# A fused attention and expert kernel: first batch in a new order, fourth batch later, a fourth buffer of scaled q, a third early unit of x sums

## The chip, the cores and the metric

One core of one Trainium2 chip. Times are device microseconds (us) of a whole execution. A ratio is the mean time of one kernel's fast runs over that of the other's fast runs of the same rounds, with a 95% interval, so it is not quite the ratio of the medians that are quoted. Times in a profile count from the start of its span, which is about 1.7 us shorter than the execution's time.

## The reference, cut to what matters

```python
# q, k, v: (8 batches, 8 heads, 576 positions, 64)
q_p = concat(relu(q) * cos, relu(q) * sin)        # the "scaled q", k_p likewise
kv  = einsum('bhsf,bhsd->bhfd', k_p, v);  z = k_p.sum(axis=2)
num = einsum('bhsf,bhfd->bhsd', q_p, kv)
den = einsum('bhsf,bhf->bhs', q_p, z)[..., None] + 1e-6
x   = (num / den) as (4608, 512)
P   = exp(x @ w_gate), 8 Sinkhorn rounds
out = sum over 8 experts e of P[:, e] * (relu(x @ w1[e]) @ w2[e])   # w1 512x1024, w2 1024x512
```

## The kernel before

TensorE works through expert 0 in blocks j = 0 to 8, each of 16 slots (8 of the first layer, 8 of the second, about 19 us). In the slots of block j the attention of batch b = j + 1 is finished and that of batch j + 2 prepared. After block 6 the buffers of the attention are freed, and experts 1 to 7 follow in a form with fewer products that works on sums of parts of x ("x sums", in units of 2 x 384 tokens). A helper `at(block, slot, fn, ...)` puts a piece of work into a slot. On TensorE, VectorE (DVE) and ScalarE (ACT) the order is the written one.

The denominators need scaled q with its features on the partitions. From batch 2 on that is done by DMA transposes issued by SyncE (SP), one for each pair of heads (hk = 0 to 3), 288 KB each. Loads of q, k and v are issued by GpSimd (POOL), six of 288 KB for a batch.

```python
kp_pool = p1.enter_context(tc.tile_pool(name="kp_pool", bufs=4))
qp_pool = p1.enter_context(tc.tile_pool(name="qp_pool", bufs=3))     # scaled q
rb_pool = p1.enter_context(tc.tile_pool(name="rb_pool", bufs=4))     # spread reciprocals
# ... cut ...
def load(b, half, names="qkv", held_back=False):
    for name in names:
        # ... cut: i = nc.gpsimd.dma_start(...)
        if held_back:
            after(ve.last, i)        # not before the DVE operation written last
        landing[name, b, half] = i

def prep_q(b, hk):
    q16 = loaded.pop(("q", b, hk))
    # ... cut: relu on DVE
    q_p = qp_pool.tile([P, C, 2, D], F16, name="q_p")
    ve.tensor_tensor(out=q_p[:], in0=..., in1=cs, op=ALU.mult)
    if by_dma:                       # b >= 2
        turned = nc.sync.dma_start(out=qTs[b, hk], in_=q_p[:]..., transpose=True)
        if b == 3 and hk == 0:
            after(landing["v", b, 1], turned)
# ... cut ...
for slot, fn, hk in (...) if j == 1 else (
    (4, prep_q, 0), (5, prep_k, 0), (5, prep_q, 1), (6, prep_k, 1),
    (8, prep_q, 2), (8, prep_k, 2), (10, prep_q, 3), (10, prep_k, 3),
    (11, prep_kv, 0), (14, prep_kv, 1),
) if j == 2 else (...):
    at(j, slot, fn, b + 1, hk)
if j == 1:
    for name in "qkv":
        for half in range(2):
            at(j, 12, load, b + 2, half, name, True)
elif j and b + 2 < B:
    for half in range(2):
        at(j, 11 + half, load, b + 2, half, "qkv", True)

def x_sums_early(n):                 # in block 6, saved to DRAM, read back later
    pool, name = ((kp_pool, "k_p"), (qp_pool, "q_p"))[n]
    # ... cut: four DVE operations, three saves
for n in range(2):
    at(B - 2, (2, 5)[n], x_sums_early, n)
```

## Time and profile before

| | before |
|---|---|
| median of 3 runs | 975.6 us (975.55 to 975.99) |
| span of the profiled run, mean clock | 972.1 us, 0.999 |
| TensorE busy | 959.4 us, 99% |
| DVE, ACT busy | 83%, 58% |

TensorE is the bound, and with 1% of idle time a change can win little. The prediction below shows the lines for the bound. Columns: start, length, engine, line, operation, output<-input, in brackets the idle time before and what ended it.

```profile
82.01 0.76 DVE L109 TENSOR_TENSOR q_p<-q_ld,acc_hi 128x1152 f16<-128x1152 f16 x1 [1.23 <-DMA q_pT<-q_p]
...
83.35 0.45 DVE L109 COPY acc_lo<-v_ld 128x576 f16<-128x576 f16 x1
...
84.10 0.72 POOL L233 DMA_DIRECT2D q_ld<-in_q_dram  x1 [13.47 <-DVE acc_lo L109]
```

DVE makes the fourth scaled q of batch 4 only when the first transpose has freed a buffer (82.01), then a copy of v (83.35), and that copy is what the loads of batch 5 are tied to (84.10). At 84.10 the fourth transpose had been issued for 1.3 us. With three buffers the fourth product cannot be made before the first transpose has landed, and the loads of batch 5 come behind that product: so the order of DVE, and the buffer it waits for, keep these loads behind the fourth transpose.

### The profile page before, as it was taken

The numbers are of one execution on the slowest core, as the hardware profiler recorded it, in microseconds if no ns is written. First come the engines' busy times: TensorE is split into PE (matmuls) and PEld (weight loads), VectorE is DVE, ScalarE is ACT, GpSimd is POOL, SyncE is SP. The second block draws the span as 40 slices with busy tenths as digits, with TensorE's granted clock in tenths as the row PEclk, the third lists the DMA queues.
The fourth block names the chain that finished last, engine by engine and source line by source line (L and its number), as shares of the span: only waits on it lengthen the run. The fifth ranks groups of instructions, "written<-read, shape, count | busy, mean of one in ns | idle before, by whom it ended". The sixth has DMA issues, their size and how long they took to land.

```text
span 972.1 us, 20258 instructions
## 1 busy us (share of the span) xinstructions
PE 959.4 (99%) x7855; PEld 674.6 (69%) x7855; DVE 807.4 (83%) x1831; ACT 565.0 (58%) x1264; POOL 60.7 (6%) x82
## 2 busy tenths in 40 slices
PE   9999999999999999999999999999999999999997
PEld 6545555567777777777777777777777777777775
DVE  7767776789898887987888987987888987987887
ACT  5767665577776555555555555555555555555551
POOL 6231210010000000000000000000000000000001
PEclk9999999999999999999999999999999999999999
DMA  9999988231004301332004301322004401115435
GB/s 162 188 154 173 156 137 184 44 69 50 26 26 93 69 25 50 68 62 57 25 26 93 69 25 51 68 54 65 26 25 86 75 25 42 33 28 124 123 90 127
DMA packets 81200, 74.72 MB, mean 77 GB/s; under 512 B 33360, under 2 KB 73040, under 8 KB 81104
## 3 DMA queue, kind: packets, MB, share of 16 engines
q0 software_dynamic: 27232, 30.94, 20.4%
q1 hardware_dynamic: 53632, 42.24, 17.8%
q8 instruction: 61, 1.00, 0.4%
q14 instruction: 35, 0.29, 0.1%
q10 hardware_dynamic: 240, 0.26, 0.1%
HBM read 84.30 MB, written 12.98 MB: 100 GB/s over the span
## 4 chain that ended last, share of the span: by engine, by line
PE 91%; DMA 4%; issue 2%; DVE 1%; POOL 1%; ACT 0%; POOLq 0%; DVEq 0%; SPq 0%; ACTq 0%
PE rows_ps L109 34%; PE h_ps L109 28%; PE p_ps L109 11%; PE copied_ps L109 11%; PE y_ps L109 4%; PE small_ps L109 3%; DMA k_ld<-in_k_dram 1%; DMA w1e<-in_moe_w_dram 1%; DMA w2e<-in_moe_w_dram 1%; DVE acc_hi L975 0%; POOL q_ld L233 0%; POOL hs_last L990 0%; DMA out_dram<-acc_lo 0%; DVE H L905 0%; DVE S L203 0%
## 5 line engine op out<-in xcount | busy, mean ns | idle before, releaser
L975 DVE SCALAR_TENSOR_TENSOR acc_lo<-rows_ps,P_tok,acc_lo 128x512 f32<-128x512 f32 (+1 forms) x322 | 203.8, 642 | 74.9 <-PE rows_ps L109 74.8
L109 PEld LDWEIGHTS <-H 128*128 128x128 f16 x2080 | 203.1, 98 | 82.3 <-issue 1.4
L911 ACT CAST u<-h_ps 128x384 f16<-128x384 f32 x288 | 137.5, 478 | 129.7 <-PE h_ps L109 129.7
L109 PEld LDWEIGHTS <-w1e 128*128 128x128 f16 x1632 | 157.7, 98 | 67.2 <-issue 5.3
L905 DVE CUSTOM_DVE_ANT_0 H<-p_ps,u 128x384 f16<-128x384 f32 x329 | 181.7, 552 | 7.2 <-PE p_ps L109 7.1
L109 PEld LDWEIGHTS <-hs 128*128 128x128 f16 x1500 | 146.6, 98 | 56.2
L109 PE MATMUL p_ps<-xT,T 128*128 128x384 f16 x672 | 164.2, 326 | 1.0 <-DVE H L905 0.9
L109 PE MATMUL h_ps<-S,w1e 128*128 128x384 f16 x672 | 164.2, 326 | 0.8 <-ACT u L911 0.6
L109 PE MATMUL rows_ps<-V,H 128*128 128x256 f16 x1000 | 150.0, 273 | 0.7 <-DVE acc_hi L975 0.7
L109 PE MATMUL rows_ps<-w2e,hs 128*128 128x256 f16 x1000 | 150.0, 273 | 0.0
L109 PE MATMUL h_ps<-xT,w1e 128*128 128x384 f16 (+1 forms) x616 | 148.8, 351 | 0.1
L943 ACT ACTIVATE H<-h_ps 128x384 f16<-128x384 f32 x144 | 70.6, 490 | 94.5 <-PE h_ps L109 94.5
L109 PEld LDWEIGHTS <-T 128*128 128x128 f16 x1008 | 98.4, 98 | 31.9 <-issue 4.9
L109 PE MATMUL rows_ps<-w2e,H 128*128 128x256 f16 (+1 forms) x568 | 94.4, 285 | 0.0
L924 ACT COPY copied_ps<-h_ps 128x384 f32<-128x384 f32 x144 | 67.5, 469 | 36.0 <-PE h_ps L109 35.2
L934 ACT ACTIVATE H<-copied_ps 128x384 f16<-128x384 f32 x144 | 70.8, 492 | 20.4 <-PE copied_ps L109 20.4
L109 PE MATMUL h_ps<-S,T 128*128 128x384 f16 x336 | 81.8, 325 | 0.6 <-ACT copied_ps L109 0.5
L109 PE MATMUL copied_ps<-xT,w1e 128*128 128x384 f16 x336 | 82.1, 326 | 0.0
L109 PE MATMUL copied_ps<-w2e,H 128*128 128x256 f16 x504 | 75.6, 273 | 0.0
L109 PE MATMUL rows_ps<-V,hs 128*128 128x256 f16 x500 | 75.0, 273 | 0.0
L975 DVE SCALAR_TENSOR_TENSOR acc_lo<-copied_ps,P_tok,acc_lo 128x256 f32<-128x256 f32 x126 | 60.3, 479 | 0.4
L975 DVE SCALAR_TENSOR_TENSOR acc_hi<-rows_ps,P_tok,acc_hi 128x512 f32<-128x512 f32 (+1 forms) x56 | 41.4, 739 | 20.6 <-PE rows_ps L109 19.7
(146 smaller groups left out, 947.7 us busy)
## 6 DMA issues: line engine op xcount, KB each, us to landing
S<-x_saved SPq DMA_DIRECT2D x114, 192.0 KB, 2.4
out_dram<-acc_lo SPq DMA_DIRECT2D x62, 128.0 KB, 2.4
w1e<-in_moe_w_dram POOLq DMA_DIRECT2D x7, 1024.0 KB, 8.8
w2e<-in_moe_w_dram POOLq DMA_DIRECT2D x7, 1024.0 KB, 9.6
q_ld<-in_q_dram POOLq DMA_DIRECT2D x16, 288.0 KB, 6.5
k_ld<-in_k_dram POOLq DMA_DIRECT2D x16, 288.0 KB, 7.8
v_ld<-in_v_dram POOLq DMA_DIRECT2D x16, 288.0 KB, 9.6
x_saved<-S SPq DMA_DIRECT2D x12, 192.0 KB, 1.8
```

What stands on the lines that cost most here:

```text
L109: i = getattr(self.engine, name)(*args, **kwargs)
L905: latest = ve._custom_dve(TENSOR_ADD_SAT, out=out, in0=ps[:, 0:TU], in1=t[:], s0=FP32_MAX, s1=0.0)
L911: se.copy(out=t[:], in_=ps[:, 0:TU])
L924: se.copy(out=Y[:, 0:TU], in_=X[:, 0:TU])
L934: se.activation(out=h11, in_=Y[:, 0:TU], func=AF.Relu)
L943: se.activation(out=h12, in_=X[:, 0:TU], func=AF.Relu)
L975: ve.scalar_tensor_tensor(out=a, in0=rows, scalar=P_tok[:, g, self.e : self.e + 1], in1=a, op0=ALU.mult, op1=ALU.add,)
```

## The change

Its intent: (A) bring the first batch to the matmuls earlier; (B) move the preparation of batch 3, the "fourth batch", later, because ACT stood at its k near 58 us, and let the loads of batch 4 follow its transposes; (C) a fourth buffer of scaled q, paid for with one of rb; (D) make the x sums of a third unit in block 6. Under (B) the preparation of batch 4 in block 2 moves to later slots too.

```diff
 C
-        qp_pool = ... bufs=3          rb_pool = ... bufs=4
+        qp_pool = ... bufs=4          rb_pool = ... bufs=3
 B
+        turnings = {}
-        def load(b, half, names="qkv", held_back=False):
+        def load(b, half, names="qkv", held_back=False, behind=None):
-                if held_back:
+                if behind is not None:
+                    after(turnings[behind], i)
+                elif held_back:
-                if b == 3 and hk == 0:
+                if b == 3:
                     after(landing["v", b, 1], turned)
+                turnings[b, hk] = turned
@@ preparation of batch 3 in block 1: k at slots 9, 10, 12, 13 (were 8, 9, 10, 12); kv of hk 0 and 1 at 13, 14 (were 10, 12)
@@ j == 2: kv of hk 2 and 3 at slots 0 and 1 (were in block 1)
@@ sums of batch 3 both at block 2, slot 2 (were block 1, slot 15 and block 2, slot 0)
@@ denominators of batch 3 at slot 4 (was 3)
@@ preparation of batch 4 in block 2
-                    (4, prep_q, 0), (5, prep_k, 0), (5, prep_q, 1), (6, prep_k, 1),
-                    (8, prep_q, 2), (8, prep_k, 2), (10, prep_q, 3), (10, prep_k, 3),
+                    (5, prep_q, 0), (6, prep_q, 1), (8, prep_k, 0), (8, prep_q, 2),
+                    (9, prep_k, 1), (10, prep_q, 3), (10, prep_k, 2), (11, prep_k, 3),
-                        at(j, 12, load, b + 2, half, name, True)
+                        at(j, 12, load, b + 2, half, name, True, (b + 1, HK - 1))
 D
-        for n in range(2):
-            at(B - 2, (2, 5)[n], x_sums_early, n)
+        for n in range(3):
+            at(B - 2, (2, 5, 9)[n], x_sums_early, n)
@@ in expert 1 the third unit is read back instead of made in place
 A (cut: some 120 lines)
+        load(0, 1, "q")               # ahead of the iota
@@ filler of the start: 110 x 64 columns instead of 74 x 128
@@ denominators ahead of the last k product, numerators interleaved with the first layer
```

More of the change, by code (lines that the diff above doesn't have):

```diff
@@ L214 @@
         kp_pool = p1.enter_context(tc.tile_pool(name="kp_pool", bufs=4))
-        qp_pool = p1.enter_context(tc.tile_pool(name="qp_pool", bufs=3))
+        qp_pool = p1.enter_context(tc.tile_pool(name="qp_pool", bufs=4))
         qT_pool = p1.enter_context(tc.tile_pool(name="qT_pool", bufs=1))
         kv_pool = p1.enter_context(tc.tile_pool(name="kv_pool", bufs=2))
-        rb_pool = p1.enter_context(tc.tile_pool(name="rb_pool", bufs=4))
+        rb_pool = p1.enter_context(tc.tile_pool(name="rb_pool", bufs=3))
         cs_pool = p1.enter_context(tc.tile_pool(name="cs_pool", bufs=1))
@@ L253 @@
         )
+        load(0, 0, "k")
         ones_sq = cs_pool.tile([P, P], F16, name="ones_sq")
@@ L261 @@
         )
-        load(0, 1, "q")
-        for name in "kv":
-            load(0, 0, name)
-            load(0, 1, name)
+        load(0, 1, "k")
+        for half in range(2):
+            load(0, half, "v")
         w0 = new_weights(wA)
@@ L287 @@
         idle_ps = ps_y.tile([P, Dm], FP32, name="y_ps")
-        for _ in range(74):
-            keep_busy(1)
+        for _ in range(110):
+            te.matmul(
+                out=idle_ps[:, 0:HP], lhsT=ones_sq[:],
+                rhs=ones_sq[:, 0:1].to_broadcast([P, HP]), start=True, stop=True,
+            )
         wrap = cs_pool.tile([P, C], FP32, name="wrap")
@@ L306, with halve @@
         ve.memset(cs_half[:], 0.0)
-        for hh in range(2):
-            ve.tensor_copy(
-                out=cs_half[hh * HP : (hh + 1) * HP, :, :, hh],
-                in_=cs[hh * HP : (hh + 1) * HP, :, :, 0],
-            )
+        def halve():
+            for hh in range(2):
+                ve.tensor_copy(
+                    out=cs_half[hh * HP : (hh + 1) * HP, :, :, hh],
+                    in_=cs[hh * HP : (hh + 1) * HP, :, :, 0],
+                )
         early = cs_pool.tile([P, 1], FP32, name="early")
@@ L320 @@
         C3 = C // 3
+        ones_col = const.tile([P, 1], FP32, name="ones_col")
+        ve.memset(ones_col[:], 1.0)
+        ones_all = const.tile([P, P], FP32, name="ones_all")
+        ve.memset(ones_all[:], 1.0)
+        eps_row = cs_pool.tile([1, 32], FP32, name="eps_row")
+        ve.memset(eps_row[:], 1e-6 / XS)
+        lent = acc_lo[:, G_LO - 4 : G_LO, :].rearrange("p g d -> p (g d)").bitcast(F16)
+        VA = C * (D + 2)
+        v_augs = [
+            lent[:, i * VA : (i + 1) * VA].rearrange("p (c d) -> p c d", d=D + 2)
+            for i in range(4)
+        ]
+        for t in v_augs:
+            ve.memset(t[:, :, D : D + 1], 1.0 / XS)
         lo = cs_pool.tile([P, 1], FP32, name="lo")
@@ L339 @@
         )
-        ones_col = const.tile([P, 1], FP32, name="ones_col")
-        ve.memset(ones_col[:], 1.0)
-        ones_all = const.tile([P, P], FP32, name="ones_all")
-        ve.memset(ones_all[:], 1.0)
-        eps_row = cs_pool.tile([1, 32], FP32, name="eps_row")
-        ve.memset(eps_row[:], 1e-6 / XS)
         wg_ld = cs_pool.tile([P, KT, E], FP32, name="wg_ld")
@@ L352 @@
         kps, qps, qTs, kvs, hls = {}, {}, {}, {}, {}
-        lent = acc_lo[:, G_LO - 4 : G_LO, :].rearrange("p g d -> p (g d)").bitcast(F16)
-        VA = C * (D + 2)
-        v_augs = [
-            lent[:, i * VA : (i + 1) * VA].rearrange("p (c d) -> p c d", d=D + 2)
-            for i in range(4)
-        ]
         q_pTs = [qT_pool.tile([P, C, P], F16, name=f"q_pT{i}")[:] for i in range(6)] + [
@@ L366 @@
         ]
-        for t in v_augs:
-            ve.memset(t[:, :, D : D + 1], 1.0 / XS)
         def prep_k(b, hk, by_scalar=True):
@@ L475, in sums, with sums_begun @@
             sums_made(b, half, sums_begun(b, half))
-        def sums_begun(b, half):
+        def sums_begun(b, half, banks=(ps_s, "small_ps")):
             W_ = D + 1 if b else D
@@ L484, in sums_begun @@
                 )
-            kv_ps = [ps_s.tile([P, 512], FP32, name="small_ps") for hh in range(2)]
+            kv_ps = [banks[0].tile([P, 512], FP32, name=banks[1]) for hh in range(2)]
             for i in range(2):
@@ L643 @@
         for hk in range(HK):
+            prep_q(0, hk)
+            if hk == 1:
+                halve()
             if hk == 3:
@@ L647 @@
                 z_ps = key_sums(0)
-                prep_q(0, hk)
-                key_sums_made(0, z_ps)
-            else:
-                prep_q(0, hk)
             for i in range(3):
                 turn(0, hk, i, True)
-                keep_busy(3)
+                keep_busy(3 * (hk < 3))
         prep_kp(0, 0)
+        key_sums_made(0, z_ps)
+        for hk in (2, 3):
+            prep_k(0, hk)
         prep_kp(0, 1)
         denominators(0, range(0, 4))
-        keep_busy(8)
-        for hk in (2, 3):
-            prep_k(0, hk)
         z_ps = key_sums(1)
+        keep_busy(4)
+        key_sums_made(1, z_ps)
         prep_kp(0, 2)
-        key_sums_made(1, z_ps)
+        denominators(0, range(4, 8))
         prep_kp(0, 3)
-        keep_busy(5)
-        denominators(0, range(4, 8))
-        for half in range(2):
-            sums_made(0, half, sums_begun(0, half))
-            keep_busy((0, 18)[half])
+        sums_made(0, 0, sums_begun(0, 0))
+        keep_busy(20)
+        spread_out(0, 0)
+        numerators(0, 0)
+        keep_busy(4)
+        spread_out(0, 1)
+        sums_made(0, 1, sums_begun(0, 1, (ps_h[0], "h_ps")))
         hT = hA.tile([P, FT, TCH], F16, name="hT")
@@ L676, with first_l1 @@
         ]
-        for hk in range(HK):
-            attend(0, hk)
-            for kt in ((), (0,), (1,), (2, 3))[hk]:
-                for ft, h_ps in enumerate(first_ps):
-                    te.matmul(
-                        out=h_ps[:],
-                        lhsT=w0[0][:, kt, ft * P : (ft + 1) * P],
-                        rhs=xT[:, kt, 0:TCH],
-                        start=(kt == 0),
-                        stop=(kt == KT - 1),
-                    )
-                    if kt == KT - 1:
-                        se.activation(out=hT[:, ft, 0:TCH], in_=h_ps[:], func=AF.Relu)
-            for i in ((), (0,), (1, 2), ())[hk]:
-                prep_k(1, i, i < 2)
-            for i in ((), (0,), (1,), (2, 3))[hk]:
-                if i == 3:
-                    prep_k(1, i, False)
-                prep_kp(1, i)
+        def first_l1(kt, fts):
+            for ft in fts:
+                te.matmul(
+                    out=first_ps[ft][:],
+                    lhsT=w0[0][:, kt, ft * P : (ft + 1) * P],
+                    rhs=xT[:, kt, 0:TCH],
+                    start=(kt == 0),
+                    stop=(kt == KT - 1),
+                )
+                if kt == KT - 1:
+                    se.activation(out=hT[:, ft, 0:TCH], in_=first_ps[ft][:], func=AF.Relu)
+        numerators(0, 1)
+        spread_out(0, 2)
+        first_l1(0, (2, 3, 0, 1))
+        numerators(0, 2)
+        spread_out(0, 3)
+        first_l1(1, range(4))
+        numerators(0, 3)
+        prep_k(1, 0)
+        prep_k(1, 1)
+        first_l1(2, range(4))
+        first_l1(3, range(4))
+        for hk in range(HK):
+            if hk >= 2:
+                prep_k(1, hk, False)
+            prep_kp(1, hk)
         for hk in range(3):
@@ L707 @@
                     for i in range(3):
-                        at(0, (5, 6, 6, 7)[hk], turn, 1, hk, i, i != 1)
+                        at(0, (6, 6, 7, 7)[hk], turn, 1, hk, i, i != 1)
                     if hk == 0:
-                        at(0, 5, prep_q, 1, 3)
-                    if hk == 2:
-                        at(0, 6, prep_v, 1, 0, se.copy)
-                        at(0, 6, prep_v, 1, 2, ve.tensor_copy)
-                    if hk == 3:
-                        at(0, 7, prep_v, 1, 1, se.copy)
-                        at(0, 7, prep_v, 1, 3, ve.tensor_copy)
+                        at(0, 6, prep_q, 1, 3)
+                    if hk in (1, 3):
+                        for i in (hk - 1, hk):
+                            at(0, (6, 7)[hk // 2], prep_v, 1, i, ve.tensor_copy)
                 for half in range(2):
@@ L737 @@
                     at(j, 5, sums, b, 1)
-                elif j == 2:
-                    at(j, 0, sums, b, 1)
                 else:
@@ L744 @@
                     at(j, 2, sums, b, 1)
-                at(j, 6 if j == 1 else 3 if j == 2 else 4, denominators, b)
+                at(j, 6 if j == 1 else 4, denominators, b)
                 for hk in range(HK):
@@ L765 @@
                 for slot, fn, hk in (
-                    (4, prep_q, 0), (5, prep_q, 1), (8, prep_k, 0), (8, prep_q, 2),
-                    (9, prep_k, 1), (10, prep_kv, 0), (10, prep_k, 2), (12, prep_q, 3),
-                    (12, prep_kv, 1), (12, prep_k, 3), (13, prep_kv, 2), (14, prep_kp, 3),
-                    (14, prep_v, 3),
+                    (4, prep_q, 0), (5, prep_q, 1), (9, prep_k, 0), (8, prep_q, 2),
+                    (10, prep_k, 1), (12, prep_q, 3), (12, prep_k, 2), (13, prep_k, 3),
+                    (13, prep_kv, 0), (14, prep_kv, 1),
                 ) if j == 1 else (
-                    (4, prep_q, 0), (5, prep_k, 0), (5, prep_q, 1), (6, prep_k, 1),
-                    (8, prep_q, 2), (8, prep_k, 2), (10, prep_q, 3), (10, prep_k, 3),
+                    (5, prep_q, 0), (6, prep_q, 1), (8, prep_k, 0), (8, prep_q, 2),
+                    (9, prep_k, 1), (10, prep_q, 3), (10, prep_k, 2), (11, prep_k, 3),
                     (11, prep_kv, 0), (14, prep_kv, 1),
@@ L779 @@
                     at(j, slot, fn, b + 1, hk, *((se.copy,) if fn is prep_v else ()))
-                if j == 1:
-                    at(j, 15, sums, b + 1, 0)
             if j == 1:
@@ L789, in x_sums_early @@
         def x_sums_early(n):
-            pool, name = ((kp_pool, "k_p"), (qp_pool, "q_p"))[n]
+            pool, name = ((kp_pool, "k_p"), (qp_pool, "q_p"))[n % 2]
             ts = [pool.tile([P, C, 2, D], F16, name=name) for _ in range(3)]
@@ L1219 @@
                 m = (n + 1) % NU
-                if e == 1 and m:
-                    if n == 0:
-                        xs_next = xs_first[1]
-                        continue
+                if e == 1 and n == 0:
+                    xs_next = xs_first[1]
+                    continue
+                if e == 1 and m > 2:
                     if i == 0:
@@ L1233 @@
                     if not (e == E - 1 and m == 0):
-                        x_again(m, xs_next)
+                        x_again(m, xs_next, saved[-1] if e == 1 and m == 2 else None)
                 if e > 1 and n == 0 and i == 0:
```

## The prediction

> **What bounds the kernel now.** I read the page first (busy times, slices), then the table of stages, then the waits of TensorE, and then the order of time around each wait.
>
> ```profile
> PE 959.4 (99%) x7855; PEld 674.6 (69%) x7855; DVE 807.4 (83%) x1831; ACT 565.0 (58%) x1264; POOL 60.7 (6%) x82
> ```
>
> ```profile
> 24.00:36.00 12.00, 10.48 (x159) 6.40 (x159) 8.10 (x18) 9.28 (x22) 4.50 (x7) 1.00 1.22 206
> 36.00:56.00 20.00, 20.00 (x225) 10.30 (x224) 17.74 (x38) 12.96 (x30) 4.30 (x6) 1.00 1.06 157
> 56.00:60.00 4.00, 2.83 (x18) 1.15 (x17) 2.04 (x6) 2.11 (x5) 0.00 (x0) 1.00 1.21 167
> 60.00:161.50 101.50, 101.43 (x1066) 52.18 (x1066) 74.59 (x169) 65.88 (x153) 18.89 (x26) 1.00 0.97 161
> 161.50:183.60 22.10, 22.10 (x128) 11.11 (x127) 16.64 (x47) 11.98 (x21) 0.00 (x0) 1.00 0.29 74
> 183.60:198.00 14.40, 13.92 (x80) 7.76 (x79) 10.70 (x25) 9.27 (x20) 0.76 (x1) 1.00 0.43 75
> 198.00:208.00 10.00, 9.01 (x58) 5.41 (x56) 9.44 (x19) 6.20 (x14) 4.03 (x3) 1.00 0.61 116
> 208.00:951.00 743.00, 742.02 (x5661) 553.08 (x5660) 637.02 (x1430) 430.57 (x964) 8.18 (x10) 1.00 0.24 56
> ```
>
> In the stage rows the columns are stretch, length, busy time of PE, weight loads, DVE, ACT, POOL, clock, DMA share, GB/s. From 60 to 161.5 us and from 208 to 951 us the matmul queue is full. The change leaves the matmuls that compute as they are (the build has the same shapes in another order; only filler differs), so it can win only where TensorE is idle or does filler: the start, 24 to 36 (1.52 us idle), 56 to 60 (1.17), 198 to 208 (0.99). A bound from spacing the matmuls at columns / 2.4 per ns says the real losses there are a little larger than the idle time: about 2.8, 1.6 and 1.5 us. Filler of the start is 18,048 columns, 7.5 us, but it fills waits and does not set them.
>
> The wait at 56 to 60:
>
> ```profile
> 57.89 0.68 ACT L109 ACTIVATE k_ld<-k_ld 128x576 f16<-128x576 f16 x1 [2.25 <-DMA k_ld<-in_k_dram]
> ...
> 58.95 0.70 ACT L109 COPY rb<-small_ps 128x384 f32<-128x384 f32 x2
> ...
> 59.48 0.46 PE L109 MATMUL small_ps<-hl,acc_hi 96*128 96x192 f16 x3 [1.11 <-ACT rb L109]
> ```
>
> ACT stands at the relu of the fourth batch's k until the load lands (57.87), with the copies that free the PSUM banks behind it.
>
> **What the Trainium skill says.** "Trainium Kernel Development and Optimization", Key Constraints: DMAs of all issuing queues run on the same 16 engines and interleave; "DMA: Bandwidth & Descriptors", Queues, rings and completion order: an engine round-robins between its queues by packet. The trace agrees: from 156 to 161 us the weights' queue and the save queue alternate, one packet of each per 0.15 us an engine, so the saves move about 150 KB/us, and the weights 115 instead of the 205 that they get alone. "TensorE: Matmul & The Clock Gate", Part 1: after an idle window of about 3.4 us the array falls to half clock, and a busy window brings it back. In this trace the clock records say full speed from 3.95 us to 969.92, 1.85 us after the last matmul ended, so a window that is partly busy can also fall; no wait inside the kernel is long enough to show it.
>
> **The change part by part.**
>
> *Start.* The second half of q is issued before the iota, the spread of cosines to halves is put behind two q products (2 copies, 0.50 us), and the denominators come before the last k product. Before: first q product 6.83, reciprocal 15.50, hl done 17.6. With the durations of before: q product 0.71 each back to back, first at about 6.0 (q landed at 5.95); k relu at about 10.2 (its load landed at 10.47; DMA is saturated, landings come every 1.4 us); 0.55 + 0.70 + 0.29 + 0.55 + 0.70 + 0.29 + 0.70 on DVE and reciprocal at about 14.2; hl done 16.2. Gain 1.4. Then four times copy of rb (0.70 on ACT) and product (0.82 on DVE), with one kv copy (0.5) between, and both engines handing PSUM banks over: last xT about 22.6, before 23.87. After it DVE has four k products, two relus, four q products, four evacuations and four v copies (two of them from ACT), in steps of 0.70, 0.27, 0.70, 0.47, 0.37: 9.5 us, to 32.1; before, the same place waited for ACT's v copy, 32.76. With 36 matmuls of sums (0.6) the first w2 matmul comes at about 32.8, before 33.78. The second w2 piece landed at 31.81, so weights allow it. **Gain 1.0 us** (0.3 to 1.8).
>
> *Fourth batch later.* Its relu of k moves from slot 8 to 9, behind the rb copies, its transposes wait for v, which frees the DMA engines for the loads (one transpose took from 53.64 to 63.81 in that crowd), and the sums of one half move to the next block. I expect the wait at 58 to go: **1.4 us**. The transposes then end about 68, and the denominators want them at about 69.5: no new wait, with 1 us to spare. The fourth scaled-q buffer takes away a DVE wait of 1.23 us at 82.01 that nothing on TensorE waited for: 0.
>
> *Third unit of x sums.* Four DVE operations of 0.55 us leave 198 to 204 and one more copy goes with the others. At 204.3 TensorE waited 0.85 us for an add on DVE, and DVE was busy for 9.44 of 10 us. In the new order another w2 difference (0.68) comes ahead of that add, so of 1.5 us of losses I count **0.8 us**.
> In block 6 the four operations fall in DVE's idle 3.12 us ahead of 159.64: no cost there. But they are saved to DRAM, three saves of 192 KB, and this is where I see the price:
>
> ```profile
> 147.86 1.79 SPq L207 DMA_DIRECT2D x_saved<-k_p  x3
> 152.37 1.51 SPq L207 DMA_DIRECT2D x_saved<-q_p  x3
> 162.62 2.76 SPq L865 DMA_DIRECT2D S<-x_saved  x6
> ...
> 162.67 0.60 ACT L109 ACTIVATE H<-h_ps 128x512 f16<-128x512 f32 x1 [0.35 <-PE h_ps L109]
> ```
>
> The H buffer of the next stage lies where the k and q products lay: in the built program ACT's first write of H waits for every save from them, in both kernels. Before, the sixth landed at 162.49, and H started at 162.67, just as the matmuls had h ready. The new saves are issued at about 157 to 158.5 behind three that end at 162.2; 24 packets an engine at 0.15 us are 3.6 us, so the last lands at about 166.1 on the old clock. TensorE has two h banks: it fills both by 163.75 and stands until the first is read at 166.9. **Loss 3.1 us.** If this wait drops the clock (more likely than not by the 1.85 us above), matmuls of a window of 3.4 us run at half speed: 1 to 1.7 us more, in expectation 0.8.
>
> Sum: 975.6 - 1.0 - 1.4 - 0.8 + 3.1 + 0.8 = 976.3. The order of the fillers looks tuned on the chip, which speaks for more gain at the start than I can trace; I take 1.3 off: **975.0 us**.
>
> **The rivals.** (a) The saves land in time, for instance because they queue more evenly over the engines: then the gains stand alone, 975.6 - 3.2 = 972.4, with a start gain of 2 us 971. For it: the last packets of the saves come from one late engine (most end at 160.9, the last starts at 162.19); against: 3.6 us of packets even on the others end past 164. (b) ACT's wait for k only moves: if the loads of the fourth batch are not faster, ACT stands one slot later; banks are then free for two slots, so at most 0.5 us. (c) The start is bound by loads, not by order: they land every 1.4 us from 5.95 to 43.1 without a break. Then the start gives 0 to 0.3, and with the wait for saves and the clock the time is 977 to 978.5. For it: DMA share 1.2 in this stretch; against: no DVE or TensorE wait after 12 us names a load.
>
> **Range and chances.** Gains 2 to 5 us, losses 0 to 5: 970.8 to 978.6 holds it eight times in ten. Two per cent is 19.5 us, far beyond both.
>
> **What would show it.** Right: ACT's first write of H near 163 to 164 waiting for a save, a TensorE idle of about 3 us after eight matmuls of stage 7, the eight or so 512-column matmuls after it at twice their 0.21 us spacing if the clock fell; the wait of 1.1 us near 57 gone; no wait for DVE near 202. Wrong: the first w2 matmul later than 33.8 or earlier than 31.8, saves that land before h is ready, or a new wait in block 2 for the fourth batch's transposes. The prediction as a whole fails if a wait that I did not find costs more than 5 us, or if the start gains more than 3.

## The result, and the profile after

The kernel after took 989.19 us (990.41, 990.68, 987.25, 987.98), against 975.63 us before in the same rounds: ratio 1.0137, interval 1.0115 to 1.0159. That is within 2%, but 13.6 us slower and far outside the predicted range. Its profiled run took 990.41 us, span 988.7, mean clock 0.992.

The table of stages, columns as in the prediction, first of the kernel before:

```profile
84.00:106.00 22.00, 22.00 (x223) 11.23 (x222) 17.25 (x40) 13.36 (x31) 8.32 (x12) 1.00 1.02 163
...
161.00:183.00 22.00, 22.00 (x128) 11.01 (x126) 16.27 (x47) 11.75 (x21) 0.00 (x0) 1.00 0.32 79
```

and of the kernel after:

```profile
56.00:60.00 4.00, 4.00 (x27) 1.82 (x28) 2.43 (x6) 3.35 (x8) 0.00 (x0) 1.00 1.11 182
...
84.00:106.00 22.00, 12.20 (x148) 5.82 (x147) 9.18 (x22) 6.83 (x15) 3.68 (x6) 0.77 0.87 128
...
161.00:183.00 22.00, 18.40 (x130) 8.96 (x127) 11.61 (x27) 9.69 (x22) 0.00 (x0) 0.92 0.94 227
```

The wait at 56 to 60 is gone, as predicted. From 84 to 106 us TensorE is busy for 12.20 of 22 us, at a clock of 0.77; from 161 to 183 it loses another 3.6 us. The first is the surprise. TensorE in order of time in the kernel after:

```profile
89.90 0.51 PE L109 MATMUL small_ps<-q_pT,zsel 128*32 128x192 f16 x12
91.76 0.34 PE L109 MATMUL small_ps<-q_pT,zsel 128*32 128x192 f16 x6 [1.34 <-DMA q_pT<-q_p]
100.33 0.51 PE L109 MATMUL small_ps<-q_pT,zsel 128*32 128x192 f16 x6 [8.23 <-DMA q_pT<-q_p]
100.77 1.89 PE L109 MATMUL h_ps<-xT,w1e 128*128 128x512 f16 x4
```

The denominators of batch 4 wait 1.34 and 8.23 us for the last two transposes of its scaled q. The clock records say half speed from 95.84 to 106.08 us: four matmuls of 512 columns take 1.89 us instead of 1.04. Of those 10.24 us some 4.5 lie in the wait itself, and in the other 5.7 half the work is lost, 2.9 us. The chain that ended last, cut to this stage (start, length, what), tells why:

```profile
71.99 10.62 DMA v_ld<-in_v_dram
...
82.63 0.04 DVE acc_lo L109
...
85.48 14.81 DMA q_pT<-q_p
100.29 0.04 issue
100.33 0.51 PE small_ps L109 x4
```

A load of v issued at 71.99 lands after 10.6 us, and a transpose issued at 85.48 takes 14.81 us. What ran beside it stands in the order of all engines of the kernel after, to be held against the three lines of before:

```profile
77.79 7.59 SPq L403 DMA_TRANSPOSE q_pT<-q_p  x2
...
78.33 0.76 DVE L109 TENSOR_TENSOR q_p<-q_ld,acc_hi 128x1152 f16<-128x1152 f16 x1
...
82.63 0.45 DVE L109 COPY acc_lo<-v_ld 128x576 f16<-128x576 f16 x1 [2.88 <-DMA v_ld<-in_v_dram]
...
83.39 0.72 POOL L234 DMA_DIRECT2D q_ld<-in_q_dram  x1 [9.97 <-DVE acc_lo L109]
```

With four buffers the fourth scaled q is ready at 79.09 and waits for nothing. But the second transpose holds SP for 5.7 us, so the third is issued at 83.62 and the fourth at 85.48. The copy of v is no longer behind a wait for a transpose; it waits only for its own load, and lets the loads of batch 5 out at 83.39, ahead of both. From issue to landing the transposes took, in the window from 70 to 101 us, in the kernel before (two of batch 5 are counted with it; the four of batch 4 alone took 4.2 to 6.0, median 5.5) and then after:

```profile
DMA to landing us min/median/max: 3.3/4.6/6.0
```

```profile
DMA to landing us min/median/max: 8.1/9.8/14.8
```

The second loss is the one that was predicted, at the first write of H in block 7 (PE in the kernel after):

```profile
178.34 4.13 PE L109 MATMUL h_ps<-xT,w1e 128*128 128x512 f16 x12 [3.60 <-ACT H L109]
```

The saves of the third unit were issued from 167.83 on and landed at 174.55, 175.87 and 177.15; ACT wrote H at 177.69, and the clock was at half from 177.76 to 181.17.

### The profile page after: what moved, and what is told of

It reads as the page before. It is cut to its first block, busy times and chain, and to the rows that moved or that the text cites. A ratio compares the mean times of both kernels' runs of the same rounds, so it can differ in the third digit from the quotient of the medians.

```text
span 988.7 us, 20313 instructions
## 1 busy us (share of the span) xinstructions
PE 963.7 (97%) x7886; PEld 675.5 (68%) x7886; DVE 808.9 (82%) x1834; ACT 564.4 (57%) x1261; POOL 60.7 (6%) x82
## 4 chain that ended last, share of the span: by engine, by line
PE 87%; DMA 7%; DVE 2%; issue 2%; POOL 1%; ACT 0%; SPq 0%; POOLq 0%; DVEq 0%; ACTq 0%
PE rows_ps L109 34%; PE h_ps L109 26%; PE p_ps L109 11%; PE copied_ps L109 11%; PE y_ps L109 3%; PE small_ps L109 2%; DMA q_pT<-q_p 1%; DMA w1e<-in_moe_w_dram 1%; DMA w2e<-in_moe_w_dram 1%; DMA v_ld<-in_v_dram 1%; DMA q_ld<-in_q_dram 1%; DMA k_ld<-in_k_dram 1%; DMA S<-x_saved 0%; DMA acc_hi<-q_p 0%; DVE acc_hi L991 0%
## 5 line engine op out<-in xcount | busy, mean ns | idle before, releaser
L109 PE MATMUL h_ps<-xT,w1e 128*128 128x384 f16 (+1 forms) x616 | 152.4, 357 | 3.7 <-ACT H L109 3.6
L109 PE MATMUL copied_ps<-xT,w1e 128*128 128x384 f16 x336 | 82.1, 326 | 0.0
```

What stands on the lines that cost most here:

```text
L109: i = getattr(self.engine, name)(*args, **kwargs)
```

## The experiments

Eighteen kernels, each beside runs of the kernel before (medians 975.2 to 975.7 us). Issue and landing times are those of the transfers in the trace. The expectations give some waits as the time beyond what the columns of the matmuls need, so they differ by a few tenths of a us from the waits of the trace. This table gathers what the trace says of the kernels that matter for block 3; "b4" is batch 4, the waits are TensorE's in blocks 2 and 3, half clock leaves out the first and last microseconds:

| kernel | loads b4: first issue, last landing | transposes b4: first, last landing | loads b5: first issue | waits of TensorE over 1 us | half clock |
|---|---|---|---|---|---|
| before | 66.33, 80.78 | 81.92, 87.00 | 84.10 | none | none |
| after | 69.14, 84.62 | 85.43, 100.29 | 83.39 | 1.34 + 8.23 (transposes b4) | 10.2 + 3.4 us |
| e1 | 62.45, 79.50 | 87.97, 94.64 | 92.71 | 9.21 (transposes b3) | 13.7 + 3.4 |
| e3 | 69.68, 81.76 | 84.32, 88.44 | 86.51 | 2.24 (DVE, block 2) | 3.4 |
| e5 | 70.01, 85.00 | 85.83, 89.13 | 89.69 | 4.01 (ACT for k) | 3.4 + 3.4 |
| e7 | 66.39, 82.58 | 84.33, 97.70 | 80.43 | 6.72 + 1.25 (transposes b4) | 10.2 + 3.4 |
| e11 | 66.34, 79.74 | 83.29, 86.19 | 84.74 | 1.12 (ACT for k) | none |
| e14 | 66.18, 78.97 | 81.54, 84.75 | 83.02 | none | none |

### First call: undo one part at a time

My first theory was that the hold on the loads of batch 4 (`behind`) made them late, so that they starved the transposes. The rivals were the later slots and the fourth q buffer.

**e1_no_hold**

```diff
-  at(j, 12, load, b + 2, half, name, True, (b + 1, HK - 1))
+  at(j, 12, load, b + 2, half, name, True)
```

> The kernel after, but the loads of batch 4 are no longer held behind the last transpose of batch 3; they wait only for the DVE operation before them in program order, as in the kernel before. Theory (the hold makes the loads of batch 4 late, so that they and then the loads of batch 5 starve the transposes of batch 4, for which the denominators of batch 4 wait 9.6 us in block 3): the loads are issued near 63 us instead of 69.1, all six have landed by about 77, the four transposes of batch 4 land before 88, the wait of 1.34 + 8.23 us and the 10.2 us of half clock after it are gone; a new wait of up to 3 us can come near 70, where the transposes of batch 3 now meet these loads. Time 972 to 977 us, 12 to 17 less than after. Rivals (later slots of the preparation in block 2, or the fourth q buffer): the loads change nothing that matters and the time stays at 987 to 991.

Measured 989.4 us (988.26 to 990.48), ratio 1.014. The loads did come at 62.45 and the wait in block 3 went, but TensorE now stood in block 2, for the transposes of batch 3:

```profile
79.61 0.51 PE L109 MATMUL small_ps<-acc_lo,zsel 128*32 128x192 f16 x6 [9.21 <-DMA acc_lo<-q_p]
```

The pile-up had only changed place. The hold is not a mistake: with loads that can come this early it protects the transposes of batch 3. The theory fell as it stood.

**e2_prep_slots**: the slots of block 2 as before (first eight pairs of the list shown in the diff).

> The kernel after, with the preparation of batch 4 in block 2 at the slots that it had before (q products at 4, 5, 8, 10, k relus at 5, 6, 8, 10). Rival 1 (the later slots put the transposes late): the wait in block 3 shrinks by most of its 9.6 us and the time falls to 972 to 980 us. Theory: the q data of batch 4 land at 73.3 and 74.7 us whatever the slots are, so the transposes start at most 1 us earlier and still meet the loads; wait 8 to 10 us, time 986 to 991.

Measured 984.11 us (982.53 to 986.14). The transposes went out at 74.1, 77.6, 82.1 and 83.5, the last landed at 90.56, and no wait for a transpose was left; but the k relus, early again, met loads that are later than before, and ACT blocked TensorE:

```profile
78.56 0.39 PE L109 MATMUL y_ps<-w2e,hT 128*128 128x512 f16 x1 [3.38 <-ACT hT L109]
```

The time is 2 us below the 986 to 991 that I expected and above the 972 to 980 of the rival, but on the wait the rival was right: without the later slots it is gone. How is not fully separated, because the stand of ACT also delays DVE's fourth product (82.42, in after 78.33), and with it batch 5's loads. The third and fourth transposes go out 1.5 and 2.0 us earlier than in after, and so ahead of batch 5's loads (84.51). The cost of it is in the early slots of k, which want loads that are not there yet.

**e3_three_q**

```diff
-  qp_pool bufs=4, rb_pool bufs=3
+  qp_pool bufs=3, rb_pool bufs=4
```

> The kernel after, with three buffers of scaled q and four of rb as before. Rival 2 (with the fourth buffer the transposes and the work behind them come closer together and pile up): the wait in block 3 goes, 972 to 978 us. Theory: the transposes are starved by the loads, and the buffer only decides when the fourth may be issued; with three it waits for the first to land (85.4), issued at most 0.5 us later than now (85.48), so the loads of batch 5, which go out behind DVE work, move by as much or a little more; wait 8 to 10 us, time 986 to 991.

Measured 980.81 us (978.78 to 984.95), 8.4 us less than after; my expectation was wrong, and the rival right about the wait, though the time stayed over its 972 to 978. In order of all engines:

```profile
84.41 0.76 DVE L109 TENSOR_TENSOR q_p<-q_ld,acc_hi 128x1152 f16<-128x1152 f16 x1 [3.25 <-DMA q_pT<-q_p]
...
86.51 0.72 POOL L234 DMA_DIRECT2D q_ld<-in_q_dram  x1 [12.52 <-DVE acc_lo L109]
```

DVE stands 3.25 us for a transpose again, and the loads of batch 5 come 3.1 us later than in after. The transposes landed by 88.44 instead of 100.29.

**e4_two_units**

```diff
-  for n in range(3): at(B - 2, (2, 5, 9)[n], x_sums_early, n)
+  for n in range(2): at(B - 2, (2, 5)[n], x_sums_early, n)
@@ third unit in place in expert 1 again
```

> The kernel after, with x sums of two units in block 6 as before, and the third and later ones in place in expert 1. Theory: the wait of 3.77 us at 174.4 for the saves of the third unit and the 3.4 us of half clock after it (1.7 us) are gone, the wait in block 3 stays; the 0.8 us that I credited to the third unit near 204 us are not lost, because the wait of 1.0 us there was still there in the kernel after. Time 982.5 to 985 us, 4.5 to 6 less than after. Rival (the saves would have been hidden if block 3 had not shifted everything; the wait is only the first late landing of a queue that stays crowded, by weights of expert 1): another wait takes its place and the time falls by under 2 us.

Measured 983.6 us (982.18 to 984.78), 5.6 us less than after, as expected. The wait for H and the fall behind it are gone, block 3 is unchanged (a wait of 8.32 us until 100.73 for the last transpose).

### Second call: is it the loads of batch 5?

**e5_hold_fifth**

```diff
-  at(j, 11 + half, load, b + 2, half, "qkv", True)
+  at(j, 11 + half, load, b + 2, half, "qkv", True, (b + 1, HK - 1) if j == 2 else None)
```

> My theory of the first four runs is half refuted: without the hold the same wait came one block earlier (9.38 us at 70.2 instead of 8.40 at 91.9), and with three q buffers it went (980.8 us), there because DVE stood 3.25 us for a transpose and the loads of batch 5, which go out behind DVE's work, came 3 us later (86.5 instead of 83.4). New theory: a set of transposes must not run beside the loads of the next batch but one; in the kernel after, the fourth q buffer lets DVE run on, so that the loads of batch 5 are issued at 83.4, ahead of the third and fourth transposes. This run is the kernel after with the loads of batch 5 held behind the last transpose of batch 4, all else left. Expected: four transposes of batch 4 landed by 89 instead of 100.3, the wait of 8.4 us and the half clock at 95.8 gone. But the loads go out at about 88.5 and k lands near 94.5, and ACT has its relu in slots 3 and 4 of block 3 (about 90 to 92), so up to 4 us of wait can come there. Time 976 to 981 us, 8 to 13 less than after. Rival (the loads of batch 4 alone starve the transposes): the fourth transpose still lands after 95, time 986 to 990.

Measured 985.52 us (984.26 to 986.73): the mechanism as expected, the size not. All four transposes had landed by 89.13, although the loads of batch 4 ran until 85.00 beside them, so batch 5's loads are what delays the last ones in the kernel after. In their place ACT stood for the k of batch 5:

```profile
95.38 0.68 ACT L109 ACTIVATE k_ld<-k_ld 128x576 f16<-128x576 f16 x1 [5.25 <-DMA k_ld<-in_k_dram]
```

TensorE waited 4.01 us behind it, and the clock fell for one more window of 3.4 us, which I had left out.

**e6_hold_fifth_slots**: the same, with `if j == 2` of the later slots made `if j in (2, 3)`.

> As the run before, with the preparation of batch 5 in block 3 at the later slots that block 2 has (k relus at 8 to 11 in place of 3, 4, 7, 10). Theory: the wait of ACT for k in block 3 is not there; what is left over before is the wait for the saves and its clock fall at block 7 (5.4 us, measured by the run with two units), less about 2.5 us of gain at the start and near 58. Time 976 to 979 us. Rival (later slots only shift the pile-up to block 4): 980 to 990 us with a wait for a transpose near 110.

Measured 983.08 us (980.63 to 983.78), over the expected 976 to 979. ACT's wait went, but DVE stood 3.4 us for the q of batch 5 and TensorE waited 3.02 us for DVE, until 100.40. Here the loads of batch 5, 5 us later than in before (89.09), were paid for in another place.

**e7_hold_earlier**

```diff
-  name, True, (b + 1, HK - 1))
+  name, True, (b + 1, 1))
```

> The kernel after, but the loads of batch 4 are held behind the second transpose of batch 3 instead of the fourth: issued at about 65.8 to 69.4 (after: 69.14 to 72.71; before: 66.33 to 69.88), and the loads of batch 5 as in after. The last two transposes of batch 3 (issued 63.8 and 65.4) land before the data of the loads flow. Theory: the loads of batch 4 land by about 81, the transposes of batch 4 go out by 82.5 and meet only the first of batch 5's loads, which come at about 83.4; last landing by 88 to 90 as in before (87.0). Wait in block 3 under 2 us, no clock fall there, time 976 to 980 us. Rival (the hold's place does not matter, because with four q buffers the loads of batch 5 always overtake): wait 5 to 10 us, time 983 to 990.

Measured 987.71 us (987.59 to 990.37); the rival was right. The loads of batch 4 are as early as before (66.39), and so everything behind them: the loads of batch 5 go out at 80.43, ahead of the third transpose at 81.11, which takes 14.8 us.

```profile
95.98 0.51 PE L109 MATMUL small_ps<-q_pT,zsel 128*32 128x192 f16 x6 [6.72 <-DMA q_pT<-q_p]
```

So with four buffers neither hold alone will do.

**e8_start_alone**: the kernel before with part A only.

> The kernel before with only the new order of the first batch (B, C and D undone). Prediction on record: gain 1.0 us (0.3 to 1.8), read off the trace of after as 1.15 us at the end of block 1. Expected 974.2 to 975.0 us, with the wait of 1.27 us near 58 either still there or moved with the k load. Rival (the start is bound by loads, so that the gain is swallowed by a wait for k or v in block 1 or 2): 975.3 to 977 us.

Measured 975.24 us (973.32 to 976.36), ratio 0.9987 with an interval from 0.9954 to 1.002: too wide to show a gain of 1 us; the median lies between the expectation and the rival. Its one profile has a span of 971.6 us, a start that is ahead (first matmul of the second layer at 32.60 against 33.78 in before), and a wait of 1.54 us for ACT, until 58.66, that is still there.

### Third call: parts alone, and both holds

**e9_four_q_alone**: the kernel before with 4 and 3 buffers.

> The kernel before with only four buffers of scaled q and three of rb. In the prediction on record I gave this part 0 us: it takes away a DVE wait of 1.23 us at 82.0 that nothing on TensorE waited for. Theory now: that wait was what kept the loads of batch 5 (issued at 84.10, behind DVE's work) away from the last two transposes of batch 4 (issued 80.92 and 82.83, landed 86.03 and 87.00). Without it the loads go out at about 82.5 to 83, the last transpose lands at 88 or later (up to 95), and the denominators of batch 4, due near 92, wait 0 to 3 us. Time 975.5 to 980 us, and the issue of the loads at least 1 us earlier. Rival (the part is worth nothing, as the prediction had it): the loads go out at 84 as before and the time is within 0.5 us of before.

Measured 975.04, 984.39, 975.63 and 985.27 us. The profiled run is the first, and in it the loads of batch 5 are issued at 84.88, later than in before: the expected step is not in it.

```profile
82.79 0.76 DVE L109 TENSOR_TENSOR q_p<-q_ld,acc_hi 128x1152 f16<-128x1152 f16 x1
84.88 0.72 POOL L233 DMA_DIRECT2D q_ld<-in_q_dram  x1 [13.80 <-DVE acc_lo L109]
```

DVE waits for no transpose here, and yet the fourth transpose is issued at 83.61, as soon as its product is made, and the loads follow it by 1.27 us, just as in before (82.83 and 84.10). SP was free; in the kernel after, it issued that transpose 6.4 us after the product was ready. So taking the wait away lets the loads overtake only where SP is held up. Two runs of four are 10 us long with a clock of 0.995 and 0.994.

**e10_three_q_two_units**: after with three q buffers and two units, so A and B only.

> The kernel after without its four q buffers and its third unit (only the new start and the later fourth batch left). From single undoings: 989.2 - 8.4 (three q) - 5.6 (two units) = 975.2 us if the two losses are separate; expected 974.5 to 976.5. No half clock between the first microseconds and the end. If they overlap: 977 to 980 us. The wait of 2.4 us at 63.6, which came with three buffers beside the later transposes of batch 3, should be there again.

Measured 977.17 us (975.71 to 979.68), 2.0 us over the 975.2 of separate losses, so they overlap a little; together the two undoings give back 12.0 of 13.6 us. What is left are the waits of DVE for transposes that three buffers bring, 8.9 us in two waits: TensorE waits 1.87 us until 65.66 and 2.29 us until 88.26, with one stretch of 3.4 us at half clock in the profiled run. So A and B without the other parts gain nothing over the kernel before (ratio 1.0019, interval 1.0004 to 1.0035).

**e11_both_holds**

```diff
@@ after with two units
-  name, True, (b + 1, HK - 1))
+  name, True, (b + 1, 1))
-  at(j, 11 + half, load, b + 2, half, "qkv", True)
+  at(j, 11 + half, load, b + 2, half, "qkv", True, (b + 1, 1) if j == 2 else None)
```

> A version that is meant to beat both: the kernel after with two units, the loads of batch 4 held behind the second transpose of batch 3 (issued at 66.4) and the loads of batch 5 held behind the landing of the second transpose of batch 4 (so issued at about 84, as in before, instead of 80.4 to 83.4). Theory: every transpose of batch 4 has landed by 88, k of batch 5 lands at about 90 to 91, just about when ACT wants it; no wait over 1.5 us in blocks 2 and 3, no fall of the clock; 972.5 to 975.5 us, 0 to 3 us under before. If the loads of batch 5 are now too late for ACT: a wait of 2 to 4 us near 90, 976 to 980 us.

Measured 973.57 us (971.51 to 974.13), ratio 0.9976, interval 0.9962 to 0.999: a little faster than the kernel before, as expected. One small wait is left, ACT for k:

```profile
91.45 0.68 ACT L109 ACTIVATE k_ld<-k_ld 128x576 f16<-128x576 f16 x1 [2.35 <-DMA k_ld<-in_k_dram]
```

**e12_third_unit_alone**: the kernel before with part D only.

> The kernel before with only the third unit of x sums in block 6. Theory: the saves of the third unit land after h of block 7 is ready, wait of 3 to 4 us at the third h tile of block 7, a window or more of half clock after it (1.7 us each), and no gain near 204: 980 to 982 us, as the undoing in the kernel after gave 5.6 us. Rival (the third unit costs only where the rest of the kernel has shifted): 975 to 977 us.

Measured 980.89 us (980.55 to 983.49), 5.6 us more than before, the same price as in after. The saves were issued at 157.3 to 158.5 and the last landed at 166.63; TensorE:

```profile
167.82 5.13 PE L109 MATMUL h_ps<-xT,w1e 128*128 128x512 f16 x12 [3.61 <-ACT H L109]
```

The profile puts ACT's wait down to a transfer that reads the saves back, but the first of those landed at 167.80, after ACT had begun to write H at 167.17; the last save landed 0.54 us before that, in the kernel after 0.54 us too.

### Fourth and fifth call: what the buffer does alone

**e13_fifth_hold_only**: e11 with the loads of batch 4 held as in after.

> The winning version (973.6 us) with the loads of batch 4 held as in the kernel after (behind the fourth transpose of batch 3, issue at 69.1 instead of 66.3). Theory: they land by 84.6 instead of 79.7, so the transposes of batch 4 end near 88 and the second, which releases the loads of batch 5, at about 86.4 instead of 84.2: k of batch 5 lands at 93 to 94 and ACT, which wants it at 89, waits 2 us longer than in the winner, with perhaps a window of half clock. 975 to 979 us. Rival (only the hold on batch 5 counts): 973 to 974.5 us.

Measured 977.12 us (974.94 to 977.93). Batch 4's loads land 5.6 us later than in e11, the release of batch 5's 2.9 us later, ACT waits 3.0 us for k and TensorE 1.79. The place of the first hold is worth 3.5 us.

**e14_later_k**

```diff
@@ e11, block 3 only
-  (3, prep_k, 0), (4, prep_k, 1),
+  (5, prep_k, 0), (5, prep_k, 1),
```

> The winning version with the first two k relus of batch 5 in slot 5 of block 3 instead of slots 3 and 4. In the winner ACT stood 2.35 us for k (landed 91.43) and TensorE 1.28 us for ACT behind it. Theory: that wait goes, 972 to 973 us, 0.5 to 1.3 us less. Rival: it only moves to the rb copies at slot 7 or to a later k, 973.5 us or more.

Measured 972.83 us (971.68 to 973.83), ratio 0.9967 to the kernel before, interval 0.9955 to 0.998: the lowest median of all, though its interval overlaps that of e11, and the two were not run side by side. Its stage from 84 to 106 us:

```profile
84.00:106.00 22.00, 21.76 (x287) 11.63 (x285) 15.80 (x36) 14.47 (x34) 7.62 (x11) 1.00 1.10 177
```

**e15_four_q_held**: the kernel before with 4 and 3 buffers and batch 5's loads behind the second transpose of batch 4.

> The kernel before with four q buffers and three of rb, and the loads of batch 5 held behind the second transpose of batch 4. Theory (the runs at 984 to 985 of the buffer alone are the pile-up of those loads and the transposes): the spread goes, all runs lie between 974 and 977.5 us. Rival (the spread comes from elsewhere, for instance from three rb buffers or from batch 3's transposes, the last of which landed at 74.0 in that profile, for a wait of 1.5 us): some runs stay at 982 to 986 us.

Measured 974.4, 988.8, 985.92, 989.47, 975.35 and 987.38 us: the spread stayed (989.47 is classed as slow, because it lies over 1.5% above the fastest; its mean clock is 0.990, those of the other long runs 0.993). So the hold on batch 5 does not remove the long runs. The rival's other place remained: in the profile, a short run, the loads of batch 4 are issued at 66.45, 0.15 us after the last transpose of batch 3, which then takes 6.9 us.

**e16_four_q_again**: e9 once more.

> The kernel before with four q buffers and three of rb once more, for a profile of a run near 985 us if chance gives one. Theory: such a profile has the loads of batch 5 issued before the fourth transpose of batch 4, this landing at 95 to 101, a wait of 5 to 9 us near 92 to 100 and about three windows of half clock; a run near 975 us has neither. Rival: the wait of a long run lies elsewhere.

Measured 974.98 and 975.51 us; chance gave no long run.

**e17_four_q_both_holds**: e15, and batch 4's loads behind the third transpose of batch 3.

> The kernel before with four q buffers, the loads of batch 5 held as in the run before, and the loads of batch 4 held behind the third transpose of batch 3. The hold on batch 5 alone left four of six runs at 986 to 989 us; in its one profile (a short run) the loads of batch 4 are issued 0.15 us after the last transpose of batch 3, which lands at 73.2 after 6.9 us and makes TensorE wait 1.0 us. Theory: the long runs are those in which these loads overtake that transpose, as in the run without the hold (9.4 us of wait at 70). With the hold all runs lie between 974 and 977.5 us. Rival (the long runs come from three rb buffers or elsewhere): some runs at 982 to 989 us again.

Measured 974.13 to 977.89 us, median 976.97: no long run in five, the longest 0.4 us over the range expected. In its profile ACT waits 3.4 us for the later k of batch 4. It is not faster than the kernel before (ratio 1.0008, interval 0.9996 to 1.0021).

**e18_three_rb**: the kernel before with three rb buffers and three of q.

> The kernel before with three q buffers as it has and only three rb buffers instead of four. Theory (the fourth q buffer is what lets the loads come too close): all runs between 974.5 and 977.5 us, as before. Rival (fewer rb buffers hold the numerators or the rb copies back and shift the prep): some runs at 982 to 989 us, or all of them over 978 us.

Measured 975.21 us (974.46 to 975.79). On the kernel before, three rb buffers cost nothing.

## Why the prediction was wrong

- **Start, predicted 1.0 us.** (Its seven DVE steps give 13.98 for the reciprocal, not 14.2, which changes little.) In the profiles the second layer of block 1 starts 1.15 us earlier (54.84 in before, 53.69 in after), and the first matmul of the second layer comes at 32.46 in after (33.78 in before, 32.8 predicted), so the estimate seems right; e8 could not confirm it in whole runs.
- **Wait near 58, predicted 1.4 us.** Gone in after, as said. The version without the new losses, e14, is 2.6 us faster than before, close to the 2.4 us of these two terms together; but no run isolates the second term, and e10, with A and B alone, was not faster than before, so that agreement may be luck.
- **Third unit, predicted 0.8 us of gain.** Wrong: TensorE waits 0.84 us for DVE's add at that place in after, 0.85 in before, and 0.8 in e12. The w2 differences and h sums that stand directly ahead of that add on DVE take the same times in before and after; that they set it is my reading, and no run varied them.
- **Saves, predicted 3.1 us and 0.8 us of clock.** Right in mechanism, though from 156 to 161 us the packets of the kernel before are 140 KB/us of saves and 120 of weights, where I read 150 and 115: last save at 166.1 predicted, 166.63 measured in e12; wait 3.6 us; half clock for one or two windows of 3.4 us. In all 5.6 us (e4, e12) against 3.9: the clock fell in each of the eight profiles with the third unit (after, e1, e2, e3, e5, e6, e7, e12), and the wait was half a us longer. From the trace of after this makes an estimate of 3.6 + 1.4 = 5.0 us (half of the time from 178.34 to 181.17), from that of e12 6.0.
- **The step that failed** is a term that I set to zero: "The fourth scaled-q buffer takes away a DVE wait of 1.23 us at 82.01 that nothing on TensorE waited for: 0." I read that wait in the kernel before and asked only which engine waited for it. The loads of batch 5 are tied to a DVE copy that comes behind it, and in the new order, where the loads of batch 4 are later and the transposes hold SP, this wait is what keeps those loads off the transposes. Its removal costs 8.4 us in the kernel after (e3), 6.4 us in the kernel with two units (e4 against e10). e5 and e11 show the same from the other side: tie the loads to a transpose itself, and the wait for the transposes goes with four buffers too. The buffer does not do it alone: on the kernel before, the profiles of e9 and e16 show no such wait, and with the old slots of batch 4's preparation (e2) the wait for transposes goes as well, with four buffers. The prediction added up its parts one by one; this loss comes of two or three together. Its own sign of failure came true: a wait that it did not find cost more than 5 us, 1.34 + 8.23 us.
- **The second half of the same failure**: I checked that batch 3's transposes would land in time (they did, at 68.60 for a need at 69.97), and did not carry the held loads on to batch 4, whose transposes met both the late loads of their own batch and the loads of the next. e7 shows that the early hold alone does not help, e5 that the late hold alone leaves a wait for k, e13 against e11 that their places are worth 3.5 us.
- **The clock** was considered only for block 7. In block 3 it added about 3 us to the wait of 9.6.

In sum: of 13.6 us, undoing the fourth buffer gives 8.4, undoing the third unit 5.6, both 12.0. Putting the slots of block 2 back gives 5.1 (e2).

**Open.** The fourth buffer on the kernel before gives runs at 975 and runs at 984 to 989: 2 long of 6 alone (e9, e16), 4 of 6 with batch 5 held, none of 5 with batch 4 held too. That points to the loads of batch 4 overtaking the last transpose of batch 3, as they do in e1, but no long run was caught in a profile, and five runs are few. (The kernel before has single runs at 978.38, 979.25 and 981.28 us among its own; why is not known either.)

## What to carry to other kernels

Before a wait on an engine is called harmless, follow what is issued behind it in that engine's order, transfers above all: an idle wait can be what keeps two transfers apart. Parts of a change that are worth nothing one by one can cost much together, so read the waits again in the new order. When a buffer is added or work is moved, tie the transfers that were kept apart by accident to the event that they must follow, and check the place of the next consumer too, for a load that is held too long only moves the wait. And a save into DRAM whose buffer is about to be reused is on the path of whatever is written there next.

## What the Trainium skill lacked or had wrong

- "DMA: Bandwidth & Descriptors", Rules for kernel authors, says "A transpose next to ordinary DMAs needs nothing". That is said of correctness, and all results here were correct; it says nothing of time. In e14 the last transpose of batch 4, issued at 81.48 between the loads of two batches, took 3.27 us from issue to landing; among six loads of 288 KB one took 14.81 us in the kernel after, with four products ready at 79.09 and the last transposed at 100.29.
- I found on no page how long the issue of a transpose holds SP: 1.3 us each for the four of batch 3 in the kernel after, 3.21 us for the first of batch 4, which has only loads beside it, and 5.73 us for the second, which delays the next issue. What sets this time was not tested.
- "TensorE: Matmul & The Clock Gate", Part 1, has the fall after an idle window of about 3.4 us; that short idles can swing the clock too it says of one other kernel, without their length. Here stands shorter than a window went with a fall: 2.29 us (e10), 1.79 us (e13) and 1.46 and 0.67 us close together (e17) each with 3.4 us of half clock, while 2.24 us in e3 and 1.12 us in e11 had none. No rule comes out of these figures. The fall with the stand of 8.23 us lasted 10.24 us.
